# Fourier mixing and SoLU MLP on one core: inverse step 1 as eight 32x64 products at once, forward step 2 as two 64-row halves side by side

## The chip, the cores and the metric

One core of a Trainium2 chip. The metric is the device time of one execution in microseconds (us). The engines are TensorE (PE; its weight loads are shown as PEld), VectorE (DVE), ScalarE (ACT) and GpSimd (POOL); SyncE (SP) issues the DMAs.

## The reference

For 8 sequences of 3136 tokens and 256 channels: a Fourier transform along the sequence, a complex 256x256 mixing with bias and a soft threshold, the inverse transform, and then an MLP per token with a softmax-gated activation (SoLU) and a layer norm.

```python
X = np.fft.rfft(x, axis=1); Xr, Xi = X.real, X.imag
Yr = Xr @ w_r - Xi @ w_i + b_r
Yi = Xr @ w_i + Xi @ w_r + b_i
Y = soft(Yr, 0.01) + 1j * soft(Yi, 0.01)      # sign(y) * max(|y| - 0.01, 0)
y = np.fft.irfft(Y, n=3136, axis=1)           # (8, 3136, 256)
h = y.reshape(25088, 256) @ w_in              # 25088 x 1024
solu = h * softmax(h)
out = (layer_norm(solu) * g_ln) @ w_out       # 25088 x 256
```

## The kernel before

The sequence length is 98 x 32, and each transform is done in two steps. Forward step 1 (`fwd1`) is a product with a 98x98 table along the first factor; it writes to DRAM (`s1`). Forward step 2 (`fwd2`) takes the 32-point transforms with their twiddle factors, `mix` multiplies by the 256x256 weights and thresholds, inverse step 1 (`inv1`) does the 32-point transforms back and writes to DRAM (`s2`), and inverse step 2 (`inv2`) does the 98-point one. The MLP follows in tiles of 128 tokens: `moe_head` (tiles ph, h and its exponentials), `moe_turn` (fp16 parts lh and ll, turned by transposing DMAs into th and tl) and `moe_tail` (po, the output product).

Frequencies come as residues k1 modulo 98. A pair of residues (real and imaginary part, 32 rows each) fills 128 rows; a *group* `u` is two such pairs, of which there are twelve in a batch, and a thirteenth (`fwd2_last`, `mix_last`, `inv1_last`) holds the residues 0 and 49. Before the change both tables are block diagonal: two residues in one 128x128 table `FB` (tiles `fb` for fp16, `fbf` for fp32) and, in a 64x128 half, two residues in `GB` (tile `gb`). Half of what they multiply is zeros.

`fwd2` handles one group: the data tile `bin` is the stationary operand, 128 rows by 128 channels, and the table moves, 128 columns. For batches 2 and up, numbers are split in two fp16 parts and three products are added, 12 matmuls to a group; batches 0 and 1 use one fp32 product, 4 matmuls, each of which the profile shows as two. All go into one PSUM bank, which ACT and DVE copy out as `Xh16` and `Xl` (fp16 high and low parts of real, imaginary and, for batches from 1 on, their sum `Xs`).

`inv1` handles two groups in a stay (one in batch 0). Its table `gb` is stationary in two halves of 64 rows, at rows 0 and 64, and the thresholded data `yh`, `yl` moves, 256 columns; two products run side by side in the two halves of the array, each into its own bank. ACT and DVE copy the banks to `zout` and SP stores it.

Bank tiles come from `Banks`: eight banks of 512 fp32, of which at most five may be `pf` (front of batches from 1 on and `inv2`), five `ph`, two `po`, and eight `pb` (batch 0's front).

Nothing is issued directly. Each operation goes to a `Plan`, which knows keys (`nc.key`, a due time in MLP tiles), operands, buffer counts and banks, simulates the engines with costs from `weigh`, and sets the order on each engine: among what may start within 50 ns of the earliest, the lowest key goes first. Operations under `nc.together()` stay together on PE. The cost of a matmul is its moving columns; those with `op.half` are priced at half, and entering or leaving that mode has a price of its own. All operations share one line in the profile (L350), so tiles tell them apart.

`front_b` sets the keys of a batch's front: in each step one `fwd2`, the `mix` of the group before and, some groups later (`lag`), `inv1`. The front of the next batch runs between the MLP tiles of the current one.

Of the kernel before, what the change touches and what calls it, by code (L numbers as in the profile page):

```python
# [39 lines left out]
def fft_constants():  # L40
# [7 lines left out]
    for q in range(Q):  # L48
        comps += [(2 * q + 1, 0), (2 * q + 2, 0), (2 * q + 1, 1), (2 * q + 2, 1)]
    comps += [(0, 0), (H, 0)]  # L50
    for c, (k1, im) in enumerate(comps):
        t = 2 * np.pi * ((np.arange(N1) * k1) % N1) / N1
        FA[:, c] = -np.sin(t) if im else np.cos(t)
        IA[c, :] = (1.0 if k1 in (0, H) else 2.0) / S * (-np.sin(t) if im else np.cos(t))

# [5 lines left out]
    for q in range(Q):  # L61
        for j in range(2):
            k = 2 * q + 1 + j + N1 * np.arange(N2)
            s = np.where(2 * k > S, -1.0, 1.0)[None, :]
            C, Sn = np.cos(angle(k)), np.sin(angle(k))
            re, im = slice(j * N2, (j + 1) * N2), slice((2 + j) * N2, (3 + j) * N2)
            FB[re, q, re], FB[im, q, re] = C, Sn
            FB[re, q, im], FB[im, q, im] = -Sn * s, C * s
            GB[re, q, re], GB[im, q, re] = C.T, -(Sn * s).T
            GB[re, q, im], GB[im, q, im] = Sn.T, (C * s).T  # L70
    kd, kn = N1 * np.arange(1, N2 // 2), H + N1 * np.arange(N2 // 2)
    nd, m = len(kd), len(kd) + len(kn)
# [16 lines left out]

    GB = GB.reshape(2, 2 * N2, Q // 2, 2, P).transpose(3, 1, 2, 0, 4).reshape(P, Q // 2, 2, P)  # L90

# [153 lines left out]
class Plan:  # L245
# [60 lines left out]
    def weigh(self, op, name, args, kw, ins, outs):  # L306
# [153 lines left out]
def fft_mix_solu_kernel(ctx: ExitStack, tc, x, w_r, w_i, b_r, b_i, w_in, w_out, g_ln, fa, fbf, fsf, iaf, fa16, fb, fs, gb, gs, ia, out):  # L460
# [20 lines left out]
    def front_psum(b):  # L481

        return banks.tile("pf" if b else "pb")
# [132 lines left out]
    def fwd1_plain(b, c):  # L616
# [13 lines left out]
        if whole:  # L630
            pool, name = (xp, "av") if b else ((fp, "zout"), (fp, "bin"), (xp, "av"))[c % 3]
            av = pool.tile([P, C1], F32, name=name, bufs=2)[:N1]
# [14 lines left out]
    QG = 4  # L647
    raw, bins = {}, {}
    s2 = {}
# [3 lines left out]
    def load_bin(b, g):  # L653
# [18 lines left out]
    def fwd2_last(b):  # L672
# [29 lines left out]
    def mix_last(b):  # L702
# [18 lines left out]
        threshold(b, y, t, c)  # L721
        yh = fp.tile([P, 2, D], F16, name="yh", bufs=4)[:, 0]
        nc.scalar.copy(yh, y)
# [24 lines left out]
    def fwd2(b, u):  # L748
        if b not in s2:
            s2[b] = dram.tile([N1, N2 * 2 * D], F16, name="s2") if b >= PLAIN_Z else dram.tile([N1, N2 * D], F32, name="s2f")  # L750
        if u == NU - 1:
            return fwd2_last(b)
        n = 2
        g, gi = divmod(2 * u, QG)
        if gi == 0:
            bins[b, g] = load_bin(b, g)
        bt, fw = bins[b, g], [(fb_s if b >= PLAIN else fbs)[g][:, gi + i] for i in range(2)]
        xh = fp.tile([P, 3, ND, 2, 2 * N2], F16, name="Xh16", bufs=3)
        xl = fp.tile([P, 3, ND, 2, 2 * N2], F16, name="Xl", bufs=3)
        xs = fp.tile([P, ND, 2, 2 * N2], F32, name="Xs", bufs=1) if b else None  # L760
        nc.reserve(xh, xl, *([xs] if b else []))

        pb = front_psum(b)
        pv = pb.rearrange("p (r h i c) -> p r h i c", r=2, h=ND, i=2)
        with nc.together():
            for i in range(n):
                for dh in range(ND):
                    ds = slice(dh * P, (dh + 1) * P)
                    if b >= PLAIN:
                        for k, (t, j) in enumerate(((0, 0), (0, 1), (1, 0))):  # L770
                            nc.tensor.matmul(pv[:, :, dh, i], bt[:, gi + i, t, ds], fw[i][:, j], start=k == 0, stop=k == 2)
                    else:
                        nc.tensor.matmul(pv[:, :, dh, i], bt[:, gi + i, ds], fw[i], start=True, stop=True)
        k = B_SCALE if b >= PLAIN else scales[b]["X"]

        if b:
            nc.scalar.activation(xs, pv[:, 1], AF.Copy, scale=k)
        nc.scalar.activation(xh[:, :2], pv, AF.Copy, scale=k)
        nc.vector.scalar_tensor_tensor(xl[:, :2], pv, k, xh[:, :2], ALU.mult, ALU.subtract)
        if b:  # L780
            nc.vector.scalar_tensor_tensor(xs, pv[:, 0], k, xs, ALU.mult, ALU.add)
            nc.scalar.copy(xh[:, 2], xs)
            nc.gpsimd.tensor_sub(xl[:, 2], xs, xh[:, 2])
        Xs[b, u] = xh, xl

# [51 lines left out]
    def mix(b, u):  # L837
        if u == NU - 1:
            return mix_last(b)
        t = mix_split(b, u) if b else mix_first(u)  # L840
        c = fp.tile([P, 2, D], F32, name="yc", bufs=2)
        y = fp.tile([P, 2, D], F32, name="y", bufs=2)
        threshold(b, y, t, c)
        yh = fp.tile([P, 2, D], F16, name="yh", bufs=4)
        yl = fp.tile([P, 2, D], F16, name="yl", bufs=4)
        nc.scalar.copy(yh, y)
        nc.gpsimd.tensor_sub(yl, y, yh)
        Ys[b, u] = yh, yl

    def inv1(b, u0, u1):  # L850


        if u0 == NU - 1:
            return inv1_last(b)
        n = 2
        half = 2 * N2
        g, gi = divmod(2 * u0, QG)
        part, dtype = ((2, D), F16) if b >= PLAIN_Z else ((D,), F32)
        if gi == 0:
            zouts[b] = fp.tile([P, QG, *part], dtype, name="zout")  # L860
        zo = zouts[b]
        w = u1 - u0
        pz = [front_psum(b) for _ in range(n)]
        nc.reserve(zo[:, gi : gi + n * w])
        with nc.together():
            for u in range(u0, u1):
                yh, yl = Ys.pop((b, u))
                for k, (t, j) in enumerate(((yh, 0), (yl, 0), (yh, 1))):
                    for ri in range(2):
                        for i in range(n):  # L870
                            rows = slice(i * half, (i + 1) * half)
                            nc.tensor.matmul(
                                pz[i][:, (u - u0) * D : (u - u0 + 1) * D], gb_s[g][rows, u % 2, ri, j], t[rows, ri], start=k + ri == 0, stop=k + ri == 3
                            )
        m = n * w
        for i in range(n):
            pv = pz[i][:, : w * D].rearrange("p (u e) -> p u e", u=w)
            if b < PLAIN_Z:
                zv = zo[:, gi : gi + m].rearrange("p (u i) e -> p u i e", i=n)[:, :, i]
                nc.scalar.activation(zv, pv, AF.Copy, scale=Z_SCALE)  # L880
                continue
            zv = zo[:, gi : gi + m].rearrange("p (u i) t e -> p u i t e", i=n)[:, :, i]
            nc.scalar.activation(zv[:, :, 0], pv, AF.Copy, scale=Z_SCALE)
            nc.vector.scalar_tensor_tensor(zv[:, :, 1], zv[:, :, 0], -LOW, pv, ALU.mult, ALU.add)
        if b >= PLAIN_Z:
            zo = zo.rearrange("p q t e -> p q (t e)")
        v = s2[b][: 4 * Q].rearrange("(q c) m -> q (c m)", c=4).rearrange("q (r m) -> r q m", r=P)
        nc.sync.dma_start(v[:, g * QG + gi : g * QG + gi + m], zo[:, gi : gi + m])

# [225 lines left out]
    for g in range(Q // QG):  # L1115
        fb_s[g] = const.tile([P, QG, 2, P], F16, name=f"fb{g}")
        gb_s[g] = const.tile([P, QG // 2, 2, 2, P], F16, name=f"gb{g}")

# [92 lines left out]
    def front_b(b, key, step):  # L1211

        lag = 4 if b == 0 else 3
        for n in range(NU + lag):
# [76 lines left out]
```

## Time and profile before

| | |
|---|---|
| median of 3 runs | 1609.48 us (1608.43 to 1612.35) |
| profiled execution | 1612.18 us, of which the span is 1610.3 us |
| granted PE clock, mean over the span | 0.987 |
| PE busy | 1568.2 us (97%) |
| DVE, ACT, POOL busy | 1318.1, 1235.7, 1115.7 us (82%, 77%, 69%) |
| DMA | 290.58 MB, mean 180 GB/s |
| matmul records | 12954 |

PE is busy through all of the span but the start: of the 40 slices of the profile it is below 90% in the first, the third and the last.

```profile
PE   5979999999999999999999999999999999999998
```

Each digit is a slice of 40.3 us in tenths; 9 is 90% or more. The printed duration of a matmul holds its way through the array, and the next one starts before it has ended, so the time that a matmul takes from PE is read from the distance of starts in the timeline.

### The profile page before, as it was taken

To read this page: it belongs to the slowest core of one execution; us is meant where nothing else is said; L and a number is where in the kernel's file an instruction comes from. 1 tells how busy PE (TensorE), PEld (TensorE's weight loads), DVE (VectorE), ACT (ScalarE), POOL (GpSimd) and SP (SyncE) were. 2 spreads that over 40 slices of the span, in tenths; PEclk is the share of its full clock that TensorE was granted. 3 is DMA by queue.
4 is the path that set the end of the run, shared out by engine and by line. 5 is a ranking of instruction groups with operands and counts; after the bars stand their busy time and mean duration, and the time that the engine had idled before them with its cause. 6 is when DMAs were issued, how large, how long until landed. Compare 5 with 4: busy or idle time off the path is not lost.

```text
span 1610.3 us, 37810 instructions
## 1 busy us (share of the span) xinstructions
PE 1568.2 (97%) x12954; PEld 1119.7 (70%) x12954; DVE 1318.1 (82%) x3417; ACT 1235.7 (77%) x2554; POOL 1115.7 (69%) x1882
## 2 busy tenths in 40 slices
PE   5979999999999999999999999999999999999998
PEld 3645877668766787667776687766876677766675
DVE  4788689996899869998788978899688878877775
ACT  4577677886788857988679867898678867788886
POOL 0545777669766678667776687766876677776776
PEclk8988999999999999999999999999999999999999
DMA  8876885898589965999669985699857976578765
GB/s 236 268 250 177 178 190 137 219 264 166 114 165 256 214 154 116 204 252 205 133 126 227 266 168 132 139 247 245 161 128 163 200 155 152 118 158 145 142 127 117
DMA packets 534904, 290.58 MB, mean 180 GB/s; under 512 B 427794, under 2 KB 504948, under 8 KB 534712
## 3 DMA queue, kind: packets, MB, share of 16 engines
q1 hardware_dynamic: 534712, 288.18, 79.1%
q8 instruction: 101, 1.65, 0.4%
q14 instruction: 91, 0.75, 0.1%
HBM read 108.25 MB, written 77.07 MB: 115 GB/s over the span
## 4 chain that ended last, share of the span: by engine, by line
PE 85%; DVE 5%; DMA 4%; ACT 3%; issue 2%; POOL 1%; SPq 0%; DVEq 0%; ACTq 0%; POOLq 0%
PE po L350 29%; PE ph L350 27%; PE pf L350 25%; PE pb L350 4%; DVE u L350 1%; DVE nm L350 1%; ACT u L350 1%; DMA zt<-in_w_r_dram 1%; DMA tl<-ll 1%; DVE av L350 1%; ACT lh L350 1%; ACT junk L350 1%; DVE xl L350 0%; POOL ll L350 0%; DMA zt<-s2f 0%
## 5 line engine op out<-in xcount | busy, mean ns | idle before, releaser
L350 POOL TENSOR_TENSOR ll<-u,lh 128x1024 f16<-128x1024 f32 x196 | 427.1, 2179 | 101.2 <-ACT lh L350 99.3
L350 PE MATMUL po<-wout,th 128*128 128x256 f16 x3136 | 374.5, 273 | 4.0 <-DMA th<-lh 2.4
L350 PEld LDWEIGHTS <-th 128*128 128x128 f16 x3136 | 305.3, 98 | 64.4 <-DMA th<-lh 4.8
L350 ACT ACTIVATE u<-ph,m,hsb 128x512 f32<-128x512 f32 x384 | 296.4, 779 | 63.3 <-DVE m L350 61.4
L350 DVE TENSOR_REDUCE nm<-ph 128x1 f32<-128x512 f32 x392 | 264.4, 683 | 71.4 <-PE ph L350 70.2
L350 DVE SCALAR_TENSOR_TENSOR u<-ph,ch,u 128x512 f32<-128x512 f32 x392 | 281.8, 747 | 26.3 <-ACT u L350 14.2
L350 PE MATMUL ph<-win_hi,ring_hi 128*128 128x512 f16 x768 | 292.4, 381 | 2.3 <-DVE u L350 2.2
L350 PE MATMUL ph<-win_lo,ring_hi 128*128 128x512 f16 x768 | 291.9, 380 | 0.0
L350 PE MATMUL ph<-win_low,ring_lo 128*128 128x512 f16 x768 | 291.8, 380 | 0.0
L350 ACT CAST lh<-u 128x1024 f16<-128x1024 f32 x196 | 206.0, 1051 | 56.8 <-DVE u L350 54.6
L350 PEld LDWEIGHTS <-ring_hi 128*128 128x128 f16 x1536 | 147.8, 98 | 143.8 <-issue 8.5
L350 ACT ACTIVATE junk<-u,total 128x1024 bf16<-128x1024 f32 x196 | 226.6, 1156 | 7.7 <-POOL total L350 7.4
L350 PE MATMUL po<-wout,tl 128*128 128x256 f16 x1568 | 203.4, 273 | 1.1 <-DMA tl<-ll 1.0
L350 PEld LDWEIGHTS <-tl 128*128 128x128 f16 x1568 | 151.2, 98 | 34.1 <-DMA tl<-ll 2.6
L350 POOL TENSOR_TENSOR y<-yt,yc 128x512 f32<-128x512 f32 (+1 forms) x104 | 131.3, 1265 | 61.0 <-ACT yt L350 33.9
L350 PE MATMUL pf<-w_hi,Xh 128*128 128x256 f16 x532 | 145.0, 273 | 0.8 <-DVE yt L350 0.7
L350 PE MATMUL pf<-w_hi,Xl 128*128 128x256 f16 x532 | 145.0, 273 | 0.5 <-DVE Xl L350 0.4
L350 PE MATMUL pf<-w_lo,Xh 128*128 128x256 f16 x532 | 145.0, 273 | 0.0
L350 PEld LDWEIGHTS <-ring_lo 128*128 128x128 f16 x768 | 75.2, 98 | 91.5 <-issue 1.4
L350 POOL TENSOR_TENSOR yl<-y,yh 128x512 f16<-128x512 f32 x96 | 112.9, 1178 | 35.0 <-ACT yh L350 34.0
L350 ACT ACTIVATE o<-po,r 128x256 f32<-128x256 f32 x196 | 93.4, 477 | 55.7 <-PE po L350 35.9
L350 PEld LDWEIGHTS <-Xh 128*128 128x128 f16 x1168 | 111.1, 98 | 24.3 <-issue 2.2
(198 smaller groups left out, 2901.6 us busy)
## 6 DMA issues: line engine op xcount, KB each, us to landing
xt<-in_x_dram SPq DMA_DIRECT2D x108, 392.0 KB
zt<-s SPq DMA_DIRECT2D x56, 392.0 KB
s<-zout SPq DMA_DIRECT2D x42, 512.0 KB
s<-av SPq DMA_DIRECT2D x48, 392.0 KB
bin<-s SPq DMA_DIRECT2D x36, 512.0 KB
out_dram<-o SPq DMA_DIRECT2D x128, 96.0 KB
out_dram<-o SPq DMA_DIRECT2D x136, 64.0 KB
bin<-s1f SPq DMA_DIRECT2D x12, 512.0 KB
```

Source lines behind the costliest of these rows:

```text
L350: getattr(engine, name)(*args, **kw)
```

## The change

The tables lose their zeros. `FB` becomes 64 rows per residue: residue j of a pair sits in rows 64j to 64j + 63 and its table has 64 columns. A product of 128 rows and 128 columns becomes two products of 64 rows and 64 columns, one in each half of the array and each into its own bank. `fwd2` now handles two groups at a time, 48 fp16 matmuls (16 in fp32) and two banks; `Xh16` and `Xl` are twice as large and have two buffers instead of three. The copies out of PSUM are done bank by bank, and the sum is cast and subtracted once for both groups.

`GB` becomes 32 rows by 64 columns per residue. `inv1` issues eight products at once: four row parts of 32 (four banks) and two column parts of 64 (two groups), 48 matmuls for two groups. For batches from 1 on four groups share a stay (`stay`), for batch 0 two. Each row part yields a quarter of the rows in its own bank; two `zout` tiles are filled and stored with one DMA each, `zout` has three buffers and `yh`, `yl` have five instead of four. The order of components in `fft_constants` follows, so that the DRAM layouts match. `op.half` in the planner is now 8 for `gb` and 2 for `fb` and `fbf`, and divides the price of the matmul.

```diff
-            op.half = "gb" in ins[0].tile.kw["name"]
-            op.length += n / 2 if op.half else n
+            op.half = 8 if "gb" in ins[0].tile.kw["name"] else 2 if moving.tile.kw["name"][:2] == "fb" else 0
+            op.length += n / max(op.half, 1)
...
-        fbs[g] = fp.tile([P, QG, P], F32, name="fbf", bufs=2)
+        fbs[g] = fp.tile([P, QG, 2 * N2], F32, name="fbf", bufs=2)
...
 def fwd2(b, u):
-        xh = fp.tile([P, 3, ND, 2, 2 * N2], F16, name="Xh16", bufs=3)
-        xl = fp.tile([P, 3, ND, 2, 2 * N2], F16, name="Xl", bufs=3)
+        xh = fp.tile([P, 3, NA, 2, N2], F16, name="Xh16", bufs=2)
+        xl = fp.tile([P, 3, NA, 2, N2], F16, name="Xl", bufs=2)
...
-        pb = front_psum(b)
+        pb = [front_psum(b) for _ in range(2)]
         with nc.together():
-            for i in range(n):
+            for i in range(QG):
                 for dh in range(ND):
...
-                            nc.tensor.matmul(pv[:, :, dh, i], bt[:, gi + i, t, ds], fw[i][:, j], start=k == 0, stop=k == 2)
+                    for k, (t, h) in enumerate(((0, 0), (0, 1), (1, 0)) if b >= PLAIN else ((0, 0),)):
+                        for j in range(2):
+                            rows = slice(j * half, (j + 1) * half)
+                            x, w = (bt[rows, i, t, ds], fb_s[g][rows, i, h]) if b >= PLAIN else (bt[rows, i, ds], fbs[g][rows, i])
+                            to = pb[j].rearrange("p (r a c) -> p r a c", r=2, a=NA)[:, :, a]
+                            nc.tensor.matmul(to, x, w.rearrange("p (r c) -> p r c", r=2), start=k == 0, stop=b < PLAIN or k == 2)
...
+        for j in range(2):
+            pv = pb[j].rearrange("p (a c) -> p a c", c=N2)
+            vh, vl = (x.rearrange("p r a j c -> p (r a) j c")[:, : 2 * NA, j] for x in (xh, xl))
+            if b:
+                nc.scalar.activation(xs[:, :, j], pv[:, NA:], AF.Copy, scale=k)
+            nc.scalar.activation(vh, pv, AF.Copy, scale=k)
+            nc.vector.scalar_tensor_tensor(vl, pv, k, vh, ALU.mult, ALU.subtract)
+            if b:
+                nc.vector.scalar_tensor_tensor(xs[:, :, j], pv[:, :NA], k, xs[:, :, j], ALU.mult, ALU.add)
...
-def inv1(b, u0, u1):
+def inv1(b, u0, n):
...
-        pz = [front_psum(b) for _ in range(n)]
+        pz = [front_psum(b) for _ in range(4)]
...
+            for w in range(nw):
+                ys = [Ys.pop((b, u0 + 2 * w + v)) for v in range(2)]
+                for k, (t, j) in enumerate(((0, 0), (1, 0), (0, 1))):
                     for ri in range(2):
+                        for v in range(2):
+                            u = u0 + 2 * w + v
+                            for i in range(4):
+                                rows = slice(i * N2, (i + 1) * N2)
+                                nc.tensor.matmul(
+                                    pz[i][v * half : (v + 1) * half, w * D : (w + 1) * D],
+                                    gb_s[u // 2][rows, u % 2, ri, j],
+                                    ys[v][t][rows, ri],
+                                    start=k + ri == 0,
+                                    stop=k + ri == 3,
+                                    tile_position=(i * N2, v * half),
+                                )
...
-        nc.sync.dma_start(v[:, g * QG + gi : g * QG + gi + m], zo[:, gi : gi + m])
+        for i, zo in enumerate(zs):
+            at = (2 * st + i) * QG
+            nc.sync.dma_start(v[:, at + slots.start : at + slots.stop], zo[:, slots])
...
 def front_b(b, key, step):
-        lag = 4 if b == 0 else 3
+        lag, stay = (4, 2) if b == 0 else (3, 4)
...
-            if u == NU - 1 or 0 <= u < NU and b == 0:
-                inv1(b, u, u + 1)
-            elif 0 < u < NU and u % 2:
-                inv1(b, u - 1, u + 1)
+            if u == NU - 1:
+                inv1(b, u, 1)
+            elif u >= 0 and u % stay == stay - 1:
+                inv1(b, u - stay + 1, stay)
```

How the instructions stand. On PE at the start of batch 0's front (`Xh` is stationary in the mixing, `w_hi` moves), before:

```order
L350 MATMUL pb<-ident,top 1x98
L350 MATMUL pb<-v,ones 128x2
L350 MATMUL pb<-fbf,bin 128x2x64 x12
L350 LDWEIGHTS Xh_319
L350 MATMUL pb<-w_hi,Xh_319 128x512
```

and after:

```order
L360 MATMUL pb<-ident,top 1x98
L360 MATMUL pb<-v,ones 128x2
L360 MATMUL pb<-fbf,bin 128x2x32 x32
L360 LDWEIGHTS Xh_327
L360 MATMUL pb<-w_hi,Xh_327 128x512
```

Three groups of 4 matmuls stood ahead of the first mixing; now two stays of 16, which are four groups, with half the columns each.

On ACT, the copies of one fp16 forward step of a batch in the middle, before:

```order
L350 ACTIVATE u,se_15674<-ph,m,hsb 128x512
L350 ACTIVATE Xs<-pf 128x256
L350 ACTIVATE Xh_15711<-pf 128x512
L350 CAST yh<-y 128x512
L350 CAST Xh_15711<-Xs 128x256
```

and after:

```order
L360 CAST yh<-y 128x512
L360 ACTIVATE Xs<-pf 128x8x32
L360 ACTIVATE Xh_16864<-pf 128x16x32
...
L360 ACTIVATE o<-po,r 128x256
L360 CAST lh<-u 128x1024
L360 CAST Xh_16864<-Xs 128x512
L360 ACTIVATE junk,var<-u,total 128x1024
```

The rows `Xs` and `Xh` stand twice in a row there, once for each bank (the second pair is left out above), and the cast of the sum once for both groups.

On ACT, the copies of one inverse stay, before:

```order
L350 CAST Xh_16003<-Xs 128x256
L350 ACTIVATE o<-po,r 128x256
L350 CAST yh<-y 128x512
L350 ACTIVATE zout<-pf 128x2x256 x2
L350 ACTIVATE ring_hi<-pf 128x384
L350 ACTIVATE last_hi<-pf 128x4x2
```

and after:

```order
L360 ACTIVATE o<-po,r 128x256
L360 ACTIVATE u,se_18123<-ph,m,hsb 128x512
L360 ACTIVATE zout<-pf 128x2x256 x4
L360 CAST lh<-u 128x1024
L360 ACTIVATE junk,var<-u,total 128x1024
L360 CAST yh<-y 128x512
```

Four banks are copied in a row where two were, at half as many places.

More of the change, by code (lines that the diff above doesn't have):

```diff
@@ L48, in fft_constants @@
     for q in range(Q):
-        comps += [(2 * q + 1, 0), (2 * q + 2, 0), (2 * q + 1, 1), (2 * q + 2, 1)]
+        comps += [(2 * q + 1, 0), (2 * q + 1, 1), (2 * q + 2, 0), (2 * q + 2, 1)]
     comps += [(0, 0), (H, 0)]
[L51 to L54, printed above, removed]
+    back = []
+    for c in range(4 * Q):
+        st, i, w, j, v, im = np.unravel_index(c, (Q // 8, 2, 2, 2, 2, 2))
+        back.append((4 * (4 * st + 2 * w + v) + 2 * i + 1 + j, im))
+    back += [(0, 0), (H, 0)]
+    for c in range(N1):
+        for M, (k1, im) in ((FA[:, c], comps[c]), (IA[c, :], back[c])):
+            t = 2 * np.pi * ((np.arange(N1) * k1) % N1) / N1
+            M[:] = -np.sin(t) if im else np.cos(t)
+        IA[c, :] *= (1.0 if k1 in (0, H) else 2.0) / S
     def angle(k):
@@ L70, in fft_constants @@
             GB[re, q, im], GB[im, q, im] = Sn.T, (C * s).T
+    FB = FB.reshape(2, 2, N2, Q, 2, 2, N2)
+    FB = np.stack([FB[:, j, :, :, :, j] for j in range(2)]).reshape(P, Q, 2 * N2)
     kd, kn = N1 * np.arange(1, N2 // 2), H + N1 * np.arange(N2 // 2)
@@ L752, in fwd2 @@
             return fwd2_last(b)
[L753 to L760, printed above, removed]
+        if u % 2:
+            return
+        half = 2 * N2
@@ L848, in mix @@
         Ys[b, u] = yh, yl
-    def inv1(b, u0, u1):
+    def inv1(b, u0, n):
         if u0 == NU - 1:
             return inv1_last(b)
-        n = 2
         half = 2 * N2
-        g, gi = divmod(2 * u0, QG)
+        st, w0 = u0 // 4, u0 % 4 // 2
+        nw = n // 2
         part, dtype = ((2, D), F16) if b >= PLAIN_Z else ((D,), F32)
[L859 to L862, printed above, removed]
-        pz = [front_psum(b) for _ in range(n)]
-        nc.reserve(zo[:, gi : gi + n * w])
+        if w0 == 0:
+            zouts[b] = [fp.tile([P, QG, *part], dtype, name="zout", bufs=3) for _ in range(2)]
+        zs = zouts[b]
+        pz = [front_psum(b) for _ in range(4)]
+        slots = slice(2 * w0, 2 * (w0 + nw))
+        nc.reserve(*(z[:, slots] for z in zs))
```

68 lines of the change are left out of this document (31 added, 37 removed).

## Prediction

> **What bounds the kernel now.** I read the page's busy shares first, then the stages, then what TensorE (PE) itself waited for.
>
> ```profile
> span 1610.3 us, 37810 instructions
> PE 1568.2 (97%) x12954; PEld 1119.7 (70%) x12954; DVE 1318.1 (82%) x3417; ACT 1235.7 (77%) x2554; POOL 1115.7 (69%) x1882
> ```
>
> Busy time in stages (engine busy us, granted clock, DMA share, GB/s):
>
> ```profile
> 40.00:100.00 60.00, 60.00 (x407) 35.56 (x407) 43.01 (x72) 39.98 (x79) 36.50 (x30) 0.96 0.76 246
> 160.00:400.00 240.00, 240.00 (x2040) 182.83 (x2038) 200.11 (x502) 184.23 (x380) 176.48 (x284) 1.00 0.84 193
> 600.00:800.00 200.00, 198.38 (x1723) 143.34 (x1721) 178.49 (x456) 160.85 (x336) 145.96 (x248) 1.00 0.82 182
> ```
>
> From 40 to 100 us (batch 0's front) and from 160 us on, PE has no gap worth naming, at clock 1.00 in the long part; DVE comes next with 178.49 of 200. PE's longest waits are all at the start:
>
> ```profile
> PE pb L350 <- DMA bin<-s1f: 12.3, 1, 12.3
> PE pf L350 <- DMA zt<-s2f: 9.0, 1, 9.0
> PE pb L350 <- DVE w_sc L350: 4.8, 1, 4.8
> PE po L350 <- DMA th<-lh: 2.4, 3, 1.8
> ```
>
> So PE's start-to-start spacings are the time, and a matmul slot saved is saved in full until another engine catches up. Printed durations (273 ns for 256 columns) are not slots; starts are. Three stretches of PE's timeline (start, us, instruction): an inverse stay of two groups, a forward step 2 of one group, and matmuls of 98 columns.
>
> ```profile
> 805.96 0.27 PE L350 MATMUL pf<-w_hi,Xl 128*128 128x256 f16 x1
> 806.16 0.39 PE L350 MATMUL pf<-yh,gb 64*128 64x256 f16 x4
> 806.39 0.38 PE L350 MATMUL pf<-yl,gb 64*128 64x256 f16 x4
> 807.26 0.38 PE L350 MATMUL pf<-yh,gb 64*128 64x256 f16 x4
> 807.58 0.39 PE L350 MATMUL ph<-win_hi,ring_hi 128*128 128x512 f16 x1
> ...
> 800.81 0.83 PE L350 MATMUL pf<-fb,bin 128*128 128x128 f16 x12
> 801.48 0.27 PE L350 MATMUL pf<-w_hi,Xh 128*128 128x256 f16 x1
> 801.59 0.27 PE L350 MATMUL pf<-w_lo,Xh 128*128 128x256 f16 x1
> ...
> 812.80 0.70 PE L350 MATMUL pf<-ia_s,zt 98*128 98x98 f16 x12
> 813.34 0.27 PE L350 MATMUL po<-wout,th 128*128 128x256 f16 x1
> ```
>
> A 256-column matmul takes a slot of 0.11 us (801.48 to 801.59; 109 ns below). The inverse stay has 24 matmuls. From 805.96 + 0.11 to 807.58 is 1.51 us; twelve slots of 109 ns are 1.31. So the two 64-row halves share a slot, and entering and leaving the half mode costs 0.20 together. Forward step 2 takes 0.67 us for 12 matmuls: 56 ns each for 128 columns.
>
> **The change, part by part.** How many of each there are:
>
> ```profile
> L350 PE MATMUL pf<-yh,gb 64*128 64x256 f16 x672 | 57.7, 270 | 0.0
> L350 PE MATMUL pf<-yl,gb 64*128 64x256 f16 x336 | 32.1, 269 | 0.0
> L350 PE MATMUL pb<-yh,gb 64*128 64x256 f16 x96 | 9.1, 271 | 0.0
> L350 PE MATMUL pb<-yl,gb 64*128 64x256 f16 x48 | 4.6, 269 | 0.0
> L350 PE MATMUL pf<-fb,bin 128*128 128x128 f16 x864 | 60.1, 219 | 0.3 <-DMA bin<-s 0.3
> ```
>
> *Inverse, batches 1 to 7.* 672 + 336 = 1008 matmuls are 42 stays of 24, 42 x 1.51 = 63.4 us. Now 21 stays of 96 matmuls in twelve rounds of eight. Each round still streams 256 columns, so if the eight overlap as the two do, a round is 109 ns: 0.20 + 1.31 + 0.02 (eight staggered starts instead of two) = 1.53, times 21 = 32.1. **Saves 31.3.** The staggering is read here (a window of 10 ns at the start of the stay above):
>
> ```profile
> L350 PE MATMUL pf<-yh,gb x2: 279/279/279, 806.2 to 806.2; 64*128 64x256 f16 x2
> ```
>
> Both halves start inside 10 ns: two row parts do not queue for a start. That column halves overlap too is unseen; the bounds are 109 ns a round and four times that (only two at once, as now). I take the low end, since starts and streams are separate per part where the trace can show it.
>
> The weights of each part must be in before its next round. One column takes 83 ns to load, 98 columns 124:
>
> ```profile
> L350 PEld LDWEIGHTS <-fa_s 98*98 98x98 f16 x288 | 34.8, 124 | 22.4 <-DVE last_lo L350 1.8 <-issue 0.2
> L350 PEld LDWEIGHTS pf<-ident,top 128*1 128x1 f32 x6 | 0.5, 83 | 1.3 <-ACT u L350 0.8
> ```
>
> That is 0.42 ns a column, about 27 ns for 64. Two loads on the same rows need 54 of the 109 ns: covered by the streaming. If all eight loads queued behind each other (216 ns) the cover would be gone; see the rivals.
>
> *Inverse, batch 0.* 144 matmuls are 12 stays of one group, 0.20 + 6 x 0.109 = 0.85 each, 10.2 us; now 6 stays of two groups, 0.20 + 0.65 + 0.02 = 0.87, 5.2. **Saves 5.0**: this stage has PE busy 60 of 60.
>
> *Forward, fp16 (batches 2 to 7).* 864 matmuls, 72 groups x 0.67 = 48.2 us. Now a stay of two groups issues 48 matmuls of 64 columns in 24 pairs. From 256 columns in 109 ns and 128 in 56 the line gives 29 ns for 64; the 98-column rows (0.54 us for 12, 45 ns) lie near that line. A stay: 0.20 (the mode switch, new here) + 24 x 0.029 = 0.90, times 36 = 32.4. **Saves 15.8.** Bounds: 28 ns a pair (half of 56), or 56 if halving the columns saves nothing, which is 0.20 + 1.34 = 1.54 a stay and a loss of 7. I take 29, as both neighbours lie on the line.
>
> The trace has a row against small slices (fp32, forward and inverse 2):
>
> ```profile
> 197.19 1.03 PE L350 MATMUL pf<-iaf_s,zt 98*128 98x98 f32 x8
> 198.06 1.04 PE L350 MATMUL po<-wout,tl 128*128 128x256 f16 x8
> 198.93 1.06 PE L350 MATMUL pf<-fbf,bin 128*128 128x128 f32 x8
> 199.82 0.27 PE L350 MATMUL pf<-w_hi,Xh 128*128 128x256 f16 x1
> ```
>
> *Forward, fp32 (batches 0 and 1).* 98 columns take 0.87/8 = 109 ns and 128 take 111: columns do not set this, the fp32 weight load does. So 64 columns gain nothing: as many slots as before, plus 12 stays of 0.20. **Costs 2.3.** Bounds: all slots halved (12 x 0.89 = 10.7 saved), or halves that do not overlap (21 lost). The middle stands because fp16 halves do overlap.
>
> *Around PE.* The copies out of PSUM keep their number and sizes, except that the combination of a stay is cast once at 512 elements instead of twice at 256 (42 ACT and 42 POOL instructions fewer); neither engine ends a stage, so nothing. But banks are now claimed four at a time (inverse) and two at a time (forward), of five that the front may hold. An inverse bank is free after both of these:
>
> ```profile
> L350 ACT ACTIVATE zout<-pf 128x512 f16<-128x512 f32 x84 | 46.3, 598 | 20.8 <-PE pf L350 20.8
> L350 DVE SCALAR_TENSOR_TENSOR zout<-zout,pf 128x512 f16<-128x512 f16 x84 | 54.6, 681 | 25.5 <-ACT zout L350 25.2
> ```
>
> Four banks keep DVE for 2.7 us in one burst, and the row maxima (nm) queue behind it on DVE; ACT's exponentials wait for those. The stores are now two of 512 KB in a row on SP's queue, and the transposes th and tl queue behind them. PE has matmuls of other token tiles to go on with, so I charge only the growth of what it waits today: 200 - 198.38 = 1.62 us where DVE is at 89%, or 10 over the 1260 us in which fronts run (160 to 1420). With 50/8 = 6 us less PE in 200, DVE is at 178.49/194 = 92%. I double the wait: **costs 10** (ends 0, and 35 with one eviction of 598 + 681 ns before each of 27 inverse stays). The tables fb, fbf and gb are loaded at half their size; DMA is not what PE waits for except at the start, so nothing.
>
> Sum: 31.3 + 5.0 + 15.8 - 2.3 - 10 = 39.8. The profiled execution took 1612.2 us (1610.3 span and 1.9 around it), 2.7 above the median 1609.5. 1612.2 - 39.8 = 1572.4, less 2.7: **1570**.
>
> **A page against the forward term.** The Trainium skill (TensorE: Matmul & The Clock Gate, Part 1, under "Wait — 56ns, not 53.3ns?") says that starts of matmuls never come closer than about 25 ns, however few columns. The two starts inside 10 ns above disagree for different parts of the array; for the stream as a whole no run here decides. By it a round of eight is 200 ns and a forward pair 50, and the sum before waits would be a saving of 6 us instead of 49.8.
>
> **Rivals.**
>
> *A limit on PE's instruction stream (slower).* A stay needs a weight load and a matmul for each of eight parts every 109 ns, 6.8 ns an instruction, and a forward pair 4 in 29 ns. The densest stretch in the trace is the 98-column one: 24 instructions in 0.54 us, 22.5 each, itself set by columns. For: nothing denser has been seen. Against: pairs start together. The new stays hold 21 x 192 + 6 x 96 + 36 x 96 = 8064 instructions and replace 63.4 + 10.2 + 48.2 = 121.8 us; 63 switches (12.6) and the fp32 term (2.3) leave 106.9, so it turns to a loss above 13.3 ns an instruction. At 18, half way to 22.5, it costs 38: 1648. Chance 0.15.
>
> *Column halves take turns.* Only the four row parts overlap, or the eight loads queue: a round is 218 ns. Inverse stay 2.82 (saves 21 x 0.20 = 4), batch 0 1.51 (saves 2), forward full: 4 + 2 + 15.8 - 2.3 - 3 of waits = 17, 1593. Speaks for it: no row has two parts on the same rows. Chance 0.12.
>
> *One start at a time (near no change).* If starts share one port, each of the 4032 matmuls of the new stays (21 x 96 + 6 x 48 + 36 x 48) costs the port's slot, and with 14.9 of switches and fp32 the break-even is 106.9/4032 = 26.5 ns. Half of today's 56 ns slot, 28, gives +6: 1615. Against it are the two starts inside 10 ns. Chance 0.04. The Trainium skill's 25 ns (page and section above) would put this rival at -6, 1603.
>
> *The gain is given back in waits.* Banks make PE wait 1.28 us at 27 inverse stays (35) and 0.4 at 36 forward stays (14): the 49.8 is gone, 1609. PE's tiny waits today speak against it, DVE at 92% for it. Chance 0.05.
>
> **How the numbers follow.** Forecast 0.64 (1556 to 1586: waits between 0 and 25). 0.3%, about what this kernel's measurement tells from no change, is 4.8 us. Faster: 0.64 + 0.12 = 0.76. Same: the waits, and half of the port, since 1603 and 1615 lie on both sides of the bound, 0.07. Slower: 0.15 + 0.02 = 0.17. The range 1554 to 1608 holds the forecast, the turns and the port's lower half, about 0.8; its ends come from waits of 0 with a part of the fp32 bound, and from the waits' upper end.
>
> **What would show it.** In the profile after: inverse stays of about 1.53 us for 96 matmuls, 109 ns from round to round; forward stays of 0.90 for 48; fp32 forward slots still 110 ns. PE still over 95% of the span; its waits behind DVE and bank copies grown by about 10 us. A round at 200 or more, or a forward stay over 1.34, breaks the main terms; inverse stays right and the time not fallen would mean waits.

## The result, and the profile after

The changed kernel takes 1583.43 us (median of 4 runs, 1580.52 to 1585.12), against 1610.76 us for the kernel before on the same chip (4 runs, 1608.43 to 1612.35). The ratio is 0.983, 95% interval 0.9809 to 0.985: 27.3 us faster. The profiled execution took 1583.23 us. The forecast was 1570, in a range of 1554 to 1608: the direction and the range held, and half as much again was expected as came. In the experiments one execution of fwd_only and one of noclip_before took over 1800 us at a clock of 0.84, and the medians below leave these two out.

The page of the kernel after, span, TensorE (PE) in 40 slices, and busy time of the engines:

```profile
span 1581.3 us, 42092 instructions
PE 1528.8 (97%) x15162; PEld 1078.8 (68%) x15162; DVE 1316.8 (83%) x3417; ACT 1227.7 (78%) x2512; POOL 1104.2 (70%) x1840
PE   5988999999999999999999999999999999999998
```

PE has 2208 matmuls more and is busy for 39.4 us less, but the span fell by 29.0 only. First the stays, on PE's timeline of the kernel after (start, us, instruction): an inverse stay of four groups, a forward fp16 stay of two groups, and a forward fp32 stay of two groups.

```profile
451.43 0.38 PE L360 MATMUL ph<-win_low,ring_lo 128*128 128x512 f16 x1
451.74 0.42 PE L360 MATMUL pf<-yh,gb 32*64 32x256 f16 x16
451.98 0.40 PE L360 MATMUL pf<-yl,gb 32*64 32x256 f16 x16
452.20 0.62 PE L360 MATMUL pf<-yh,gb 32*64 32x256 f16 x32
452.63 0.40 PE L360 MATMUL pf<-yl,gb 32*64 32x256 f16 x16
452.85 0.40 PE L360 MATMUL pf<-yh,gb 32*64 32x256 f16 x16
453.19 1.92 PE L360 MATMUL po<-wout,th 128*128 128x256 f16 x16
...
598.66 0.38 PE L360 MATMUL ph<-win_lo,ring_hi 128*128 128x512 f16 x1
598.88 0.38 PE L360 MATMUL ph<-win_low,ring_lo 128*128 128x512 f16 x1
599.19 0.87 PE L360 MATMUL pf<-fb,bin 64*128 64x64 f16 x48
599.99 0.28 PE L360 MATMUL pf<-w_hi,Xh 128*128 128x256 f16 x1
...
213.14 0.38 PE L360 MATMUL ph<-win_low,ring_lo 128*128 128x512 f16 x1
213.45 2.00 PE L360 MATMUL pf<-fbf,bin 64*128 64x64 f32 x32
215.39 0.28 PE L360 MATMUL pf<-w_hi,Xh 128*128 128x256 f16 x1
```

A 512-column matmul keeps its slot for 0.22 us (598.66 to 598.88). So the inverse stay lasts from 451.43 + 0.22 to 453.19, 1.54 us for 96 matmuls. From the start of the third round to that of the eleventh, 451.98 to 452.85, eight rounds take 0.87: 109 ns a round of eight. The forward stay goes from 599.10 to 599.99: 0.89 us for 48 matmuls. The fp32 stay goes from 213.36 to 215.39: 2.03 us, where two stays of one group took 1.78 before.

In the inverse stay a window of 30 ns holds the starts of a whole round (tile gb):

```profile
L360 PE MATMUL pf<-yh,gb x8: 292/292/292, 451.7 to 451.8; 32*64 32x256 f16 x8
```

Eight starts in 30 ns are against the Trainium skill's rule (TensorE: Matmul & The Clock Gate, Part 1, "Wait — 56ns, not 53.3ns?") of some 25 ns between starts, as a rule for the whole stream; no run here shows it for one tile alone.

How often each occurs, by form:

```profile
L360 PE MATMUL pf<-fb,bin 64*128 64x64 f16 x1728 | 31.5, 190 | 0.5 <-DMA bin<-s 0.5
L360 PE MATMUL pf<-yh,gb 32*64 32x256 f16 x1344 | 30.3, 271 | 0.0
L360 PE MATMUL pf<-yl,gb 32*64 32x256 f16 x672 | 16.8, 268 | 0.0
L360 PE MATMUL pb<-fbf,bin 64*128 64x64 f32 x192 | 15.1, 323 | 12.2 <-DMA bin<-s1f 12.2
```

Summed over all stays from the first start to the next start behind them, and with 96 ns for each entry, the inverse takes 35.0 us less than before, the fp16 forward 15.8 less and the fp32 forward 2.8 more. That is 48.0 us of work gone from PE. The span shows 29.0 of it, so 19.0 went elsewhere. First the kernel before, then after, in the stretch in which the fronts of batches 1 to 7 run (stretch and its length, then busy us of PE, PEld, DVE, ACT, POOL, granted clock, DMA share, GB/s):

```profile
160.00:1420.00 1260.00, 1253.37 (x10843) 916.30 (x10841) 1071.62 (x2761) 989.12 (x2054) 920.02 (x1532) 1.00 0.81 180
```

```profile
160.00:400.00 240.00, 235.41 (x2443) 175.35 (x2440) 204.33 (x509) 184.29 (x376) 172.82 (x281) 1.00 0.82 186
600.00:800.00 200.00, 194.45 (x2026) 138.74 (x2022) 176.10 (x453) 159.22 (x328) 148.02 (x243) 1.00 0.84 183
160.00:1420.00 1260.00, 1240.86 (x13031) 893.08 (x13028) 1093.58 (x2838) 1008.60 (x2072) 929.65 (x1545) 1.00 0.83 183
```

PE stood idle for 6.6 of the 1260 us before (1260 - 1253.37) and for 19.1 after. At 160 to 400 there was no gap, now there are 4.6 us; at 600 to 800 1.6 us became 5.6. This idle time understates the loss: a matmul counts as busy for 0.27 us after its start where its slot is 0.11, so each wait hides its first part. By distances of starts, what goes beyond slots and stays grew from 55.1 to 74.4 us over the whole span, 19.3, of which 3.1 lie before 200 us. The clock stayed at 1.00 in that stretch.

Who released PE, longest sums of the kernel after (us, times, longest):

```profile
PE pb L360 <- DMA bin<-s1f: 12.2, 1, 12.2
PE po L360 <- DMA th<-lh: 3.6, 5, 1.5
PE pb L360 <- DVE w_sc L360: 3.1, 1, 3.1
PE pf L360 <- DVE Xl L360: 3.1, 4, 1.3
PE ph L360 <- DVE u L360: 3.0, 3, 1.2
PE pf L360 <- DVE wpeak L360: 2.9, 1, 2.9
PE pf L360 <- DMA zt<-s2f: 2.6, 1, 2.6
PE po L360 <- DVE av L360: 2.4, 2, 1.2
```

The first row is the start, as before. No row took the place of those removed: there are many small waits, of one to five occurrences, on different tiles and releasers. Added up by releaser from 160 us on, DVE went from 4.8 us (8 waits) to 11.1 (16), and DMA from 3.7 (7) to 8.2 (9).

### The profile page after: what moved, and what is told of

The parts are those of the page before. It is cut to its first block, busy times and chain, and to the rows that moved or that the text cites. A ratio compares the mean times of both kernels' runs of the same rounds, so it can differ in the third digit from the quotient of the medians.

```text
span 1581.3 us, 42092 instructions
## 1 busy us (share of the span) xinstructions
PE 1528.8 (97%) x15162; PEld 1078.8 (68%) x15162; DVE 1316.8 (83%) x3417; ACT 1227.7 (78%) x2512; POOL 1104.2 (70%) x1840
## 4 chain that ended last, share of the span: by engine, by line
PE 77%; DVE 9%; ACT 5%; DMA 4%; issue 3%; POOL 2%; SPq 0%; DVEq 0%; ACTq 0%; POOLq 0%
PE po L360 28%; PE ph L360 25%; PE pf L360 20%; PE pb L360 4%; DVE u L360 2%; DVE nm L360 1%; ACT junk L360 1%; DMA th<-lh 1%; ACT u L360 1%; DVE xl L360 1%; DVE av L360 1%; DVE yt L360 1%; POOL ll L360 1%; DMA zt<-s2f 1%; ACT av L360 1%
## 5 line engine op out<-in xcount | busy, mean ns | idle before, releaser
L360 POOL TENSOR_TENSOR y<-yt,yc 128x512 f32<-128x512 f32 (+1 forms) x104 | 128.7, 1239 | 66.5 <-DVE ll L360 31.2
```

The costliest lines, as they stand in the source:

```text
L360: getattr(engine, name)(*args, **kw)
```

## The experiments

Three theories stood for where the 19 us went. *TensorE catches up with VectorE* (A): with less PE work, DVE is late more often. *Bank claims* (B): four PSUM banks at once make PE wait for copies. *Order* (C): the planner writes one fixed order for each engine, any change of work or price gives another order, and how well it fits decides some microseconds.

In the table "idle" is 1260 minus PE's busy time at 160 to 1420 us, and "waits" what distances of starts have beyond slots and stays, over the whole span. The ratio is to the kernel before on the same chip; that kernel had medians from 1610.8 to 1611.6. The waits are those of the profiled execution, which can lie some us off the median (pat25 4.5 and old_price 3.9 below, pat100_before 3.7 above).

| kernel | median us | ratio, 95% interval | idle us | waits us |
|---|---|---|---|---|
| before | 1610.76 | | 6.6 | 55.1 |
| after | 1583.43 | 0.983, 0.9809 to 0.985 | 19.1 | 74.4 |
| inv_only | 1596.98 | 0.9923, 0.9906 to 0.994 | 17.0 | 70.3 |
| fwd_only | 1615.60 | 1.0025, 1.001 to 1.004 | 15.5 | 70.3 |
| fwd16_only | 1609.02 | 0.9987, 0.9974 to 1.0 | 14.7 | 66.5 |
| f32_whole | 1571.89 | 0.9757, 0.9743 to 0.9771 | 14.3 | 58.6 |
| pf6 | 1597.22 | 0.9914, 0.9902 to 0.9927 | 30.1 | 86.8 |
| noclip_before | 1619.93 | 1.0063, 1.0051 to 1.0075 | 12.2 | 62.6 |
| noclip_after | 1573.06 | 0.977, 0.9755 to 0.9785 | 9.9 | 63.5 |
| pat100_before | 1612.69 | 1.0009, 0.9998 to 1.002 | 8.8 | 60.2 |
| pat100_after | 1593.20 | 0.9888, 0.9866 to 0.9911 | 18.9 | 74.2 |
| pat25 | 1598.39 | 0.992, 0.9907 to 0.9933 | 21.6 | 75.8 |
| f32_price | 1596.19 | 0.9903, 0.9891 to 0.9915 | 25.5 | 73.8 |
| old_price | 1619.64 | 1.005, 1.0036 to 1.0064 | 39.8 | 100.7 |

A wait inside a stay or right behind it is counted in the stay and not in the last column; where that matters it is said below. In after the stays hold 0.9 us of such waits.

### One half of the change at a time: inv_only and fwd_only

inv_only has the new `gb`, `inv1` and `back` (the order of components on the way back) with `fwd2` as before; fwd_only has the new `fb`, `fbf` and `fwd2` with `inv1` as before. The planner's line for the two:

```diff
 inv_only
+            op.half = 8 if "gb" in ins[0].tile.kw["name"] else 0
+            op.length += n / max(op.half, 1)
 fwd_only
+            op.half = 2 if "gb" in ins[0].tile.kw["name"] or moving.tile.kw["name"][:2] == "fb" else 0
+            op.length += n / max(op.half, 1)
```

> The inverse step as in the changed kernel (eights, four groups in a stay), the forward step as before. In the trace of the changed kernel the inverse stays took 35.0 us less of TensorE than before, the forward ones 13.0 less (15.8 less in fp16, 2.8 more in fp32), and other waits took 19 back. Theory A (TensorE catches up with VectorE, so waits grow with what it saves, 19 of 48): 21 us faster, about 1590. Theory B (waits come from claiming four banks at once in the inverse step): nearly all 19 are here, 16 us faster, about 1595. Theory C (waits are luck of the order): no relation, anything from 16 to 35 faster.

> The forward step as in the changed kernel (64-row halves, two groups in a stay), the inverse step as before. Slots alone: 13 us faster. Theory A: 8 faster, about 1603. Theory B: the inverse step's banks are as before, so the full 13 faster, about 1598. Theory C: 0 to 13.

inv_only gains 14 us, fwd_only loses 4 to 5, and both together gain 27: the parts do not add up. Each is worse than any of the three theories had it: inv_only was to gain 16 us or more, fwd_only not to lose. What they save on PE does add up: the inverse stays fell from 68.5 to 38.5 us in inv_only and the fp16 forward stays from 48.3 to 29.0 in fwd_only, where after has 36.0 and 29.0. What does not is the waits: each half alone raises them by 15.2 us, both together by 19.3. So the forward half alone gives back in waits what its fp16 stays save, the inverse half gives back half, and the second half then adds only 4 us of waits. Theory B put nearly all of the waits on the inverse step, and fwd_only, whose inverse step is as before, has 15.2 us of them.

### The fp32 products whole again: f32_whole and fwd16_only

`fbf` is again a 128x128 table and one product for each group and channel half, in the new stay of two groups; everything else is as in after (f32_whole) or as in fwd_only (fwd16_only).

```diff
+                    if b < PLAIN:
+                        to = pb[a // ND // 2].rearrange("p (r a j c) -> p r a j c", r=2, a=2 * ND, j=2)[:, :, a % (2 * ND)]
+                        nc.tensor.matmul(to, bt[:, i, ds], fbs[g][:, i].rearrange("p (r j c) -> p r j c", r=2, j=2), start=True, stop=True)
+                        continue
...
-            op.half = 8 if "gb" in ins[0].tile.kw["name"] else 2 if moving.tile.kw["name"][:2] == "fb" else 0
+            op.half = 8 if "gb" in ins[0].tile.kw["name"] else 2 if moving.tile.kw["name"][:2] == "fb" and moving.dtype != F32 else 0
```

> The changed kernel, with the fp32 forward products of batches 0 and 1 whole again (128 rows and 128 columns, one after another, still two groups in a stay). If the fp32 weight load sets their slots, as in the prediction, the halves bought nothing and cost their mode switches: forward fp32 stays 2.8 us shorter in sum, the rest as the order has it: 1578 to 1583. If the halves did save, it is slower than 1583.

> Before, with the fp16 forward stays alone in two row halves, two groups in a stay, and fp32 left as whole products; the inverse is as before. Direct terms: the fp16 forward stays save 15.8 us, nothing else. If the 5 us that fwd_only lost against before came from the fp32 halves: 1594 to 1599. If the loss is the order into which the planner puts twice as long forward stays: 1605 to 1616, with the sum of TensorE's waits up by 10 us or more. If parts add up to the 39 us of f32_whole (inv_only gave 14): 1586.

Undoing the fp32 part makes after 11.5 us faster, 1571.89 (1578 to 1583 was expected), and fwd_only 6.6 us faster. So f32_whole beats both kernels, and in both surroundings the kernel without the fp32 halves is faster. Its timeline shows the direct part:

```profile
207.90 0.38 PE L361 MATMUL ph<-win_low,ring_lo 128*128 128x512 f16 x1
208.11 1.95 PE L361 MATMUL pf<-fbf,bin 128*128 128x128 f32 x16
209.90 0.27 PE L361 MATMUL pf<-w_hi,Xh 128*128 128x256 f16 x1
```

From 208.11 to 209.90 is 1.79 us for two groups, against 2.03 with halves: 0.24 for each of 12 stays, 2.9 us, near the 2.3 that the prediction gave to this term. The other 8.6 are waits: PE's idle time at 160 to 1420 us is 14.3 us instead of 19.1, and by starts the waits are 15.8 us lower, of which 7.4 come back as waits in the fp16 stays and behind them (gb 42.5 instead of 36.0 us, fb 29.9 instead of 29.0). How much of that comes with whole products and how much with a luckier order, the runs do not separate.

fwd16_only also answers what the fp16 forward part is worth alone. It has its stays as predicted (29.0 us instead of 48.3, with 3.5 for the entries), and gains 2.4 us in the median, within what can be told from no change (4.2 between the two profiled executions): 15.8 went from the stays and 11.4 came back in waits. Of its expectations the one for the order fits (1605 to 1616, waits up by 10 us or more); had the fp32 halves alone made the loss of fwd_only, it would have been 1594 to 1599.

### A bank more for the front: pf6

```diff
-    banks = Banks(..., 8, pf=5, ph=5, po=2, pb=8)
+    banks = Banks(..., 8, pf=6, ph=5, po=2, pb=8)
```

> The changed kernel with six instead of five banks allowed to the front (of the same eight). Theory B: the four-bank claims find room sooner, 8 to 15 us less waiting, 1568 to 1575. Theory A: within 3 us of 1583. Theory C: it is one more order, 5 to 12 us away to either side.

Slower than after by 13.8 us. The stretch of 160 to 1420 us and the longest waits:

```profile
160.00:1420.00 1260.00, 1229.87 (x12914) 885.39 (x12913) 1082.92 (x2807) 995.62 (x2043) 918.28 (x1515) 0.99 0.82 181
```

```profile
PE pf L360 <- DVE top L360: 8.4, 2, 7.9
PE po L360 <- DMA th<-lh: 6.6, 6, 2.4
PE po L360 <- DMA tl<-ll: 6.3, 7, 1.7
```

30.1 us idle, with more banks for the front; all three theories missed the size, and B also the direction. The waits that grew are for `top`, a batch's peak, which scales its data (one wait of 7.9 us, where after has 0.5 in all), and for the transposed th (3.6 in after) and tl (2.1 in after). None of these is a wait for a bank: the new limit let the planner write another order, and that one fits worse. The wait for `top` shows it. In pf6 the product that turns it stands on PE where DVE has not yet made it; in after the same product comes 92 us behind its `top` (348.9 us) and waits for nothing. First pf6, then after:

```profile
337.71 0.37 PE L360 MATMUL pf<-ident,top 128*1 128x128 f32 x1 [7.90 <-DVE top L360]
```

```profile
440.93 0.27 PE L360 MATMUL pf<-ident,top 128*1 128x128 f32 x1
```

Since the order changed too, pf6 alone does not say what the bank claims cost. The trace of after says more: PE has no idle time before any matmul of the inverse stays of batches 1 to 7 (0.0 in both of their rows above), and by starts nothing beyond the entry either. One wait from 160 us on is for a copy out of an inverse bank:

```profile
PE pf L360 <- DVE zout L360: 1.1, 1, 1.1
```

Waits of 1.8 us for `Xl` by products that do not read it may be for a bank of a forward stay. So bank claims are a small part of the 19 us in after, as far as its waits show it.

### Less work for VectorE: noclip_before and noclip_after

The clip in `threshold`, a DVE operation, is left out, in the kernel before and in after.

```diff
-            nc.vector.tensor_scalar(c, t, up, down, ALU.min, ALU.max)
+            c = bias_t[:, :2] if len(t.shape) == 3 else bias_t[:, 2]
```

> The kernel before with the threshold's clip left out (91 VectorE instructions, 60 us of VectorE; a constant is subtracted in its place, so the output isn't the reference's). TensorE waits little there, so all theories: 0 to 6 us faster than before, 1604 to 1611.

> The changed kernel with the same clip left out. Theory A: with VectorE 4% lighter most of the added waits go, 1566 to 1572, and the distance to the same edit of the kernel before grows from 27 to about 37. Theory B: banks are claimed as before the edit, the distance stays at 27, about 1578. Theory C: the distance changes by some us either way.

After becomes 10.4 us faster, before 9.1 us slower, where every theory had it 0 to 6 faster. noclip_after, 160 to 1420 us:

```profile
160.00:1420.00 1260.00, 1250.11 (x13091) 900.89 (x13090) 1054.26 (x2767) 1013.55 (x2085) 923.07 (x1554) 1.00 0.83 184
```

DVE has 39.3 us less in this stretch than in after (1093.58 - 1054.26), PE's idle time falls from 19.1 to 9.9, and the waits that DVE releases from 160 us on fall from 11.1 to 5.8. Alone, that would speak for VectorE's theory. But in noclip_before DVE has 44.8 us less than in before (1026.80 against 1071.62), and PE's idle time goes up from 6.6 to 12.2. Less work on an engine that released half of the waits (4.8 of 8.9 us from 160 us on) can lose 9 us: the edit also gave a new order (the product that turns batch 3's `top` stands at 327 us instead of 446). So DVE's load as the cause is consistent with one of the two runs and not shown.

### The same work in another order: pat100_before, pat100_after, pat25

Only the planner's patience is changed, the 50 ns in "what may start within 50 ns of the earliest".

```diff
-    PATIENCE = 50.0
+    PATIENCE = 100.0
```

(pat25 has 25.0, in after.)

> The kernel before with the planner's patience (among operations that may start within so many ns the lowest key goes first) at 100 instead of 50: the same work in another order. Theory A (TensorE catches up with VectorE) and theory B (four banks at once): the order matters little where TensorE waits only 15 us after the start, within 3 us of before. Theory C (the waits are a matter of the order that the planner wrote; a static order fits the real times more or less well): 5 to 12 us away from before, to either side.

> The changed kernel with patience 100. Theories A and B: within 3 us of the changed kernel (1583), as the waits come from the machine. Theory C: 5 to 12 us away from it.

> The instructions of after and its prices; only the planner's patience is 25 in the place of 50, a new order at the same fit. It sizes luck: with 100 the same kernel was 10 us slower. Theory 'luck': up to 10 us on either side of 1583, stays unchanged, the waits moving by as much as the time.

The kernel before does not move with 100 (interval 0.9998 to 1.002), as theories A and B had it; after loses 9.8 us with 100, as C had it, and 15.0 with 25. pat25, 160 to 1420 us:

```profile
160.00:1420.00 1260.00, 1238.41 (x12956) 890.55 (x12955) 1092.28 (x2817) 998.00 (x2049) 924.25 (x1525) 1.00 0.83 182
```

Its idle time is only 2.5 us above after's. By starts, the waits outside stays are 1.4 us above, and 9.4 more lie in the stays and right behind them (gb 43.4 instead of 36.0 us, fbf 28.1 instead of 26.4, fb 29.3 instead of 29.0): one inverse stay takes 5.39 us up to the next start and another 3.13, where the other nineteen take 1.45 or, once, 1.94. (The profiled execution took 1593.90 us, 4.5 below its median.) "Stays unchanged" and "up to 10 us" were misses of the expectation.

### The same work at another price: f32_price and old_price

```diff
 f32_price
-            op.length += n / max(op.half, 1)
+            op.length += n if moving.dtype == F32 else n / max(op.half, 1)
 old_price
-            op.length += n / max(op.half, 1)
+            op.length += n / 2 if op.half else n
```

> The instructions of after, all of them; only the planner's price of the fp32 halves of batches 0 and 1 is changed, from half a product to a whole one, so that a stay of 16 stands in the plan with about 1.7 us where the trace shows about 1.9 and the old price gave 0.9. Theory 'fit' (the written order pays for the 1 us by which each of 12 such stays is underpriced): 1573 to 1578, most of the 11.5 us by which the kernel with whole fp32 products was faster. Theory 'direct' (those 11.5 us are the 2.0 us of shorter fp32 stays, 2.4 us of switches and what hangs on them): 1581 to 1586. Theory 'luck' (any new order moves the time by up to 10 us either way): anything from 1573 to 1597, as likely above after as below.

> The instructions of after; the planner's price of an inverse product of eight is n/2 (before's rule) where after has n/8, so that the plan holds about 5.2 us for a stay of 96 where the trace shows 1.53, 3.7 us too much in each of 21 stays. Theory 'fit': slower than after by 8 to 25 us, with the waits up by as much and the stays unchanged (36 and 29 us). Theory 'luck': within 10 us of after on either side.

f32_price was the sharp test of one idea: that the wrong price of the fp32 halves was what f32_whole had repaired. It fell. With the better price the same instructions are 12.8 us slower than after, not 5 to 10 faster. Its longest waits from 160 to 400 us:

```profile
PE pf L360 <- DVE top L360: 5.0, 1, 5.0
PE po L360 <- DVE c L360: 4.0, 1, 4.0
```

In this stretch after's waits for these two are nothing. The first is the wait that pf6 has too, for the `top` of the same batch, the one numbered 3:

```profile
334.63 0.37 PE L360 MATMUL pf<-ident,top 128*1 128x128 f32 x1 [4.97 <-DVE top L360]
```

The stays and what stands right behind them hold more waits (fb 36.1 instead of 29.0 us, gb 39.4 instead of 36.0). A few single waits make most of the difference, and apart from this one they are at other places in each of these kernels.

old_price misprices much: the plan holds 3.7 us too much in each of 21 stays. It is 36.2 us slower than after (8 to 25 was expected) and slower than before, with the same instructions:

```profile
160.00:1420.00 1260.00, 1220.21 (x12697) 874.55 (x12696) 1078.70 (x2770) 982.07 (x2016) 897.19 (x1493) 0.99 0.81 179
```

```profile
PE po L360 <- DMA th<-lh: 11.2, 12, 2.0
PE po L360 <- DMA tl<-ll: 10.5, 12, 1.9
```

39.8 us idle, and the waits for th and tl are 12 each where after has 5 for th and 2 for tl. I read it so: PE reaches the tails of the MLP before their transposes are in, since a stay in front of them is over 3.7 us earlier than the plan has it. So in this one order the old price of eights costs more than the 27 us that the whole change brings. That a price far off costs time is shown; that a better price in a small term pays is not.

Together: after's instructions ran in five orders of the planner with sensible prices (after, pat100_after, f32_price, pf6, pat25). They took 1583, 1593, 1596, 1597 and 1598 us. The order is worth up to 15 us, by patience alone (pat25), and after's own is the best of the five. In the four others the change gains 13 to 18 us over before instead of 27; before itself was timed in one other order only, and that one made no difference.

## Why the prediction was right, and where it was not

**Inverse, batches 1 to 7 and batch 0** (31.3 and 5.0, together 36.3): measured 31.1 and 3.9, together 35.0. The round of eight is 109 ns, the stay 1.54 us for the 1.53 forecast. In batch 0 one stay took 1.65 us to the next start, the others 0.79.

**Forward, fp16** (15.8): measured 15.8; the stay is 0.89 us for 0.90, so a pair of 64 columns costs 29 ns as the line through 128 and 256 columns gave.

**Forward, fp32** (costs 2.3): measured 2.8. The weight load keeps its length (192 ns before, 188 after, for batch 1), the slot stays at about 111 ns with half the columns, and the mode switch is added. That the slot does not follow the columns is shown; that the load sets it is argued.

**The three rivals on PE fell, and the fourth came in part.** 16 instructions, a load and a matmul for each of eight parts, pass in 109 ns, 6.8 ns each, where the loss began at 13.3. A round is 109 ns and not 218, so column halves do not take turns. Eight starts lie in 30 ns, so there is no port of 26 ns, and a forward pair takes 29 ns, not 50. The gain given back in waits was to be all of it; it was 19.0 of 48.0 us, and not at the stays that this rival named.

**Batch 0's 5.0 us did not arrive as an earlier start.** The first inverse step 2 of the kernel before, and of after:

```profile
114.81 7.12 PE L350 MATMUL pf<-iaf_s,zt 98*128 98x98 f32 x32 [9.00 <-DMA zt<-s2f]
```

```profile
122.15 7.12 PE L360 MATMUL pf<-iaf_s,zt 98*128 98x98 f32 x32 [2.56 <-DMA zt<-s2f]
```

It starts 7.3 us later, but after 2.6 us of waiting instead of 9.0: other work was put in front of it (16 matmuls of xt instead of 12 behind the last inverse stay, and waits of 0.5 and 2.1 us). The stays of batch 0 are shorter, and by this reading the chain behind them (thresholds, the store, the load of zt) sets the start all the same. This is a reading of two traces; no run tested it alone.

**The step that failed is "costs 10" for the waits.** Two things in it. The rule "growth of what it waits today, doubled" was made at one window, 600 to 800 us, where 1.6 us became 5.6, 3.4 times as much and not twice. Over 160 to 1420 us this window gave 10 us of idle time for the kernel before, where its trace has 6.6; it became 19.1, and so grew by 12.5 where 10 were charged. And idle time in the profile was taken for the loss: by starts the waits grew by 19 over the span, 16 of them behind 200 us, since each wait begins under the printed end of the matmul before it. The range of this term (0 to 35) held. The four banks claimed at once, which the prediction named as a reason, made no wait in front of an inverse stay, and DVE was busy for 88% of 600 to 800 us, not 92%.

So the miss of 13.4 us is 9.0 of waits, 1.8 of stays (49.8 forecast, 48.0 measured), and 2.7 that the prediction took off because its profiled execution lay above the median; the one after lies 0.2 below its median.

**Some luck is in the total.** The terms on PE were right for their reasons, to 2 us in 50. That the time fell between 1556 and 1586, where the prediction put 0.64, also hangs on the order: the same instructions in four other orders took 1593 to 1598.

Two slips in the working change nothing: a batch 0 stay of 1.51 us would have saved 1.1 us and not 2 (so 1594 for that rival), and of the four waits said to be at the start the last, for th, lies wholly behind 160 us.

**What made the waits** is shown in part. Bank claims are a small part (the trace of after). A badly priced order makes 26 us more of them (old_price); orders at sensible prices differ by 13 outside the stays, and by 15 in time. That VectorE's load sets a floor under them is open. For it: the kernel before had 55 and 60 us of waits in two orders, after's five orders 74 to 87. Against it: f32_whole has 58.6, and 7 more in its stays, with as much work for DVE as after. A run with DVE relieved and the order held fixed would settle it, and none was made.

## What to carry to other kernels

Count the slots of TensorE from distances of starts, and look whether tiles on separate rows and columns share a slot, as they did fully here, with about 0.2 us for each stay in that mode; the fp32 product kept its slot of about 111 ns with half the columns, so there the whole product was better. Where an order is planned ahead, a change of work is a new order: keep the price of the new instructions near the measured one, time the same work in three or four orders, and trust no single run about an effect smaller than their spread, here 15 us. A saving on an engine that was never idle can come back in part as scattered small waits though no other engine is above 87% of 160 to 1420 us: here 19 of 48 us.

## What the runs showed of the hardware

- Eight 32x64 parts run at full speed together: 16 PE instructions in 109 ns, 6.8 ns each, kept up round after round (a whole stay is 192 instructions in 1.54 us, entry and exit counted). The densest stretch of the trace before had 22.5 ns an instruction.
- Column halves on the same 32 rows, each with its weight loads, do not lengthen the round of 109 ns. A load is printed with 105 ns and stays under the running round:

```profile
L360 PEld LDWEIGHTS <-gb 32*64 32x64 f16 x2304 | 30.1, 105 | 8.8 <-issue 6.7 <-DVE yt L360 0.8 <-DMA fb<-in_fb_dram 0.4
```

  The Trainium skill says that tiles work independently, loads and products in parallel (TensorEngine Tiling (Array Packing), Key Properties); rounds of 109 ns agree, also for two tiles on the same rows.
- Entering a mode costs 96 ns beyond the slot of the matmul before (598.88 to 599.19 is 0.31, less 0.215), and so it is for eight parts (451.43 to 451.74) and for fp32 halves (213.14 to 213.45).
